# Attention with two gated layers on one core: softmax sums inverted for two head pairs at once, and the first values kept on chip

## The chip, the cores and the metric

The kernel runs on one core of a Trainium2 chip. The metric is device time in microseconds (us), the median of a few runs of the whole kernel in one launch. The core's engines are called here as the profile calls them: PE (TensorE matmuls, with PEld for its weight loads), DVE (VectorE), ACT (ScalarE), POOL (GpSimd) and SP (SyncE, which here only issues transfers). Each engine works through its own instruction stream in order, and waits at an instruction whose semaphores are not there yet.

## What is computed

The reference is windowed attention (batch 2, 8 heads, 768 positions, head size 64), then a dense gated layer, then a second layer in which each token goes to one of 8 experts:

```
keep   = is_global | is_local            # first 8 positions, or the last 96
scores = scale*q@k.T + bias;  a = exp(scores - max) where keep
x      = (a / (sum(a) + 1e-9)) @ v       # 1536 tokens x 512
x      = (silu(x @ w_gate) * (x @ w_val)) @ w_out        # 512 -> 1536 -> 512
e      = argmax(x @ r_gate);  out = gate * sigmoid * relu(x @ w1[e]) @ w2[e]
```

All inputs and the output are float32. In the kernel, large products are made of a high and a low part in the format fp32r, three matmuls for one.

## The kernel before

Queries come in 12 tiles of 128 positions, six for each of the two batches; tile i is position tile t = i % 6 of batch i // 6. Because a query only looks at the last 96 positions and at the first few, a tile needs its own keys and those of the tile before (two blocks of 128), and the first 8 positions of the batch. The kernel doesn't give these first positions a block of their own. It writes the first GW = 32 keys and values of the batch over the first 32 rows of the *previous* tile's block, which lie too far back to be local for this tile. A table of biases (`tabs`) is built for that layout. So from the second tile of a batch on, two things are put in place for each tile: keys (L324 to L328, on POOL, from the copy `kgb` that was taken at the batch's first tile) and values (L390 to L391, by a transfer from HBM on SP's queue, 32 partitions x 8 heads x 64 values).

Work goes in steps: one step is one tile and one pair of heads, 48 in all. What belongs to a step is spread over five:

- `att_S` (step s): scores into two PSUM banks `ps_s0`, `ps_s1`; DVE adds the bias and takes the maximum (L346, as a minimum of negated scores) into the buffer `sp`; ACT takes the exponential and its sum `sm` (L350).
- `att_R` (s + 1): DVE adds 1e-9 to two sums (L378, shown as L174 `rs`), inverts them (L379), and POOL multiplies `sp` by the result (L380).
- `att_P` (s + 3): PE transposes `sp` (L365), ACT or DVE copies it to `pT`.
- `att_V` (s + 4): PE multiplies by the values (L396). After the fourth pair `att_X` writes the tile's tokens as `xhi` (ACT, L402) and `xlo` (DVE, L403).

Tiles 0 and 1 (8 steps) run first with filler matmuls (`spin`, L149). Then, after a pause of 4 steps (GO = 12), the first dense layer runs between the attention steps: its up-products (L446) and down-products (L478 to L480) are handed out in small portions, and in the same stretch DVE and ACT turn that layer's wide weights into float32 and split them (`wide_to_f32` and `split_raw`, L411 to L429; a unit is a piece of weights of 128 x 1024). The first up-products need `xhi` and `xlo` of tiles 0 and 1 and the first two units. Seven units fit beside attention; the others are converted when attention's memory is free. Most instructions' order on an engine is set by a scheduler that goes by its own estimate of when each is ready; those wrapped in `pin` keep their written order. Buffers matter too: `sp` has 4, `rs`, `pT` and `qr` have 2, the values `vr` have 3.

Of the kernel before, what the change touches and what calls it, by code (L numbers as in the profile page):

```python
# [20 lines left out]
P = 128  # L21
BIG = 1.0e30
GW = 32
# [10 lines left out]
def attn_moe_moe_kernel(  # L34
# [138 lines left out]
    def ts(o, a, s1, s2, o0, o1=ALU.bypass):  # L173
        return nc.vector.tensor_scalar(out=o, in0=a, scalar1=s1, scalar2=s2, op0=o0, op1=o1)  # L174
# [143 lines left out]
    def att_S(i, j):  # L318
        b, t = bt(i)
        sl, order, tb = window(i)  # L320
        nw = len(order) * P
        if j == 0 and t > 0:
            o = (i - 1) % 3
            if stacked(i):  # L324
                nc.gpsimd.tensor_copy(ks[:, o, :, 0:GW], f(kg))
            else:
                nc.gpsimd.tensor_copy(khi[:, o, :, 0:GW], f(kgh))
                nc.gpsimd.tensor_copy(klo[:, o, :, 0:GW], f(kgl))  # L328
# [41 lines left out]
            nc.vector.tensor_copy(pT[:, :, 0:n, :], pt[:, :, 0:n, :])  # L370
        pt_t[(i, j)] = pT

    def att_R(i, j):
        sl, order, tb = window(i)
        nw = len(order) * P
        sp = sp_t[(i, j)]
        rs = at_p.tile([P, 2, 1], F32, tag="rs", name="rs")
        ts(rs[:, :, 0], sm[:, i, 2 * j:2 * j + 2], 1e-9, None, ALU.add)  # L378
        nc.vector.reciprocal(rs, rs)  # L379
        nc.gpsimd.tensor_tensor(out=sp[:, :, 0:nw], in0=sp[:, :, 0:nw], in1=rs.to_broadcast([P, 2, nw]), op=ALU.mult)  # L380

    av_t = {}

    def att_V(i, j):
        b, t = bt(i)
        sl, order, tb = window(i)
        pT = pt_t.pop((i, j))
        if j == 0:
            av_t[i] = ps_tile("av", [P, NPAIR, P])
            if t > 0:  # L390
                nc.sync.dma_start(out=v_t[i - 1][0:GW], in_=v[b, :, 0:GW, :].rearrange("h p d -> p h d"))  # L391
        av = av_t[i]
        for w, src in enumerate(order):
            vt = v_t[i] if src == 0 else v_t[i - 1]
            for e in range(2):
                nc.tensor.matmul(av[64 * e:64 * e + 64, j, :], vt[:, 2 * j + e, :], pT[:, e, w, :],  # L396
                                 start=(w == 0), stop=(w == len(order) - 1))
# [465 lines left out]
    for t in range(nstep + PAUSE + 5):  # L863
        rate = (0, 0, 0) if t < GO else (1, 0, 1 + (t % 3 == 2))
        nspin = 0 if t >= GO else 10 if t < 3 else 5 if t < FIRST else 8
        new, norm, turn, mul = (step_at(t - z) for z in (0, 1, 3, 4))
        if norm:
            att_R(*norm)
        if t < NPAIR:
            scale_tab(t, 0)  # L870
        if TL <= t + 1 < NPAIR + TL:
            scale_tab(t + 1 - TL, 1)
        if new:
            att_S(*new)
        quanta(rate[0])
        spin(nspin)
        if mul:
            att_V(*mul)
            if mul[1] == NPAIR - 1:
                i = mul[0]  # L880
                att_X(i)
                if i % 2 == 1:
                    ready.add(i // 2)
                if i + 2 < NTILE:
                    load_v(i + 2)
        quanta(rate[1])
        if turn:
            att_P(*turn)
        quanta(rate[2])
        spin(nspin)  # L890
        if new and new[0] != 1:
            transposes(*new)
        elif FIRST <= t < FIRST + 2:
            transposes(1, t - FIRST)
        if t < GO:
            early(t)
        elif t < GO + 2 * NE and (t - GO) % 2 == 0:
            clear_rows((t - GO) // 2)
        elif t == GO + 2 * NE:
            split_wr()  # L900
            nc.gpsimd.tensor_copy(ids[:, NTILE - 1:NTILE], tokid[:, NTILE - 1:NTILE])
# [455 lines left out]
```

## Time and profile before

| what | us |
|---|---|
| median of 3 runs (lowest, highest) | 667.36 (666.58, 669.77) |
| the profiled execution's own time | 666.85 |
| its span on the core | 665.0 |
| PE busy, of the span | 634.8 (95%) |
| DVE busy | 437.2 (66%) |
| ACT busy | 325.6 (49%) |
| POOL busy | 134.2 (20%) |

Busy times are those of the whole span, which has several stages. Attention with its start lies between 0 and about 200 us; then come the rest of the first dense layer (to about 460 us), the routing, and the experts. A busy PE need not be at its peak, because matmuls overlap. The profile's waits name who ended an idle stretch of an engine; an idle stretch in square brackets, as [0.72 <-PE ps_s L338], stands in a timeline's row behind the instruction that followed it.

### The profile page before, as it was taken

What the parts mean: (1) busy time and instruction counts of PE and PEld (TensorE: products, weight loads), DVE (VectorE), ACT (ScalarE), POOL (GpSimd) and SP (SyncE); (2) the same over time, 40 slices, a digit from 0 to 9 for tenths busy, and PEclk for the clock granted to TensorE, in tenths of its full rate; (3) what the DMA queues carried; (4) which work ended last, traced back from release to release, by engine and by line L of the source; (5) the groups of instructions that cost most, each with busy time, mean ns of one, the idle gap of its engine ahead of it and who ended that gap; (6) DMA issues with size and microseconds to landing.
All of it is one profiled execution on the core that took longest, in us unless ns stands there. A gap on an engine that the chain in (4) does not pass through costs nothing.

```text
span 665.0 us, 11812 instructions
## 1 busy us (share of the span) xinstructions
PE 634.8 (95%) x4455; PEld 549.8 (83%) x4455; DVE 437.2 (66%) x1087; ACT 325.6 (49%) x755; POOL 134.2 (20%) x180
## 2 busy tenths in 40 slices
PE   9899999999999999999999999998979999999993
PEld 8777678888888798999999999986867888888882
DVE  6899985666677898464464535556579777876330
ACT  4777866666665553131132222233467666766230
POOL 3404644444432420000000111001311100110011
PEclk9899999999999999999999999999999999999998
DMA  8679982210015535030010111113689767662001
GB/s 219 164 196 257 191 187 64 65 36 21 22 25 192 175 129 203 1 127 1 1 65 1 63 64 64 49 61 99 204 292 316 223 234 246 221 219 95 12 27 30
DMA packets 71587, 80.84 MB, mean 122 GB/s; under 512 B 43376, under 2 KB 43376, under 8 KB 71520
## 3 DMA queue, kind: packets, MB, share of 16 engines
q1 hardware_dynamic: 64960, 57.35, 30.6%
q0 software_dynamic: 6560, 22.64, 10.1%
q8 instruction: 37, 0.61, 0.4%
q14 instruction: 30, 0.25, 0.1%
HBM read 66.31 MB, written 14.26 MB: 121 GB/s over the span
## 4 chain that ended last, share of the span: by engine, by line
PE 71%; DVE 11%; DMA 7%; issue 5%; ACT 4%; POOL 1%; POOLq 0%; SPq 0%; DVEq 0%; ACTq 0%
PE ps_gv L446 25%; PE ps_gv L971 5%; PE ps_av L396 3%; DMA raw<-in_moe_w_dram 2%; PE ps_y L480 2%; PE ps_y L971 2%; PE ps_s L971 2%; PE ps_y L479 2%; PE ps_tr L365 2%; PE ps_y L478 2%; PE ps_s L989 2%; PE ps_s L990 2%; PE ps_s L988 2%; PE ps_s L334 2%; DMA raw<-in_moe_w_val_dram 2%
## 5 line engine op out<-in xcount | busy, mean ns | idle before, releaser
L446 PE MATMUL ps_gv<-xlo,whi 128*128 128x256 f32 x576 | 164.5, 286 | 0.9 <-DVE xlo L403 0.9
L446 PE MATMUL ps_gv<-xhi,whi 128*128 128x256 f32 x576 | 164.8, 287 | 0.3 <-DVE hh L454 0.2
L446 PE MATMUL ps_gv<-xhi,wlo 128*128 128x256 f32 x576 | 164.8, 286 | 0.0
L446 PEld LDWEIGHTS ps_gv<-xlo,whi 128*128 128x128 f32 x576 | 110.0, 191 | 4.7 <-DVE xlo L403 1.3
L446 PEld LDWEIGHTS ps_gv<-xhi,whi 128*128 128x128 f32 x576 | 109.7, 191 | 4.5 <-ACT xhi L402 0.5
L446 PEld LDWEIGHTS ps_gv<-xhi,wlo 128*128 128x128 f32 x576 | 110.2, 191 | 1.5 <-issue 0.3
L635 DVE TENSOR_TENSOR wlo<-raw,whi 128x512 fp32r<-128x512 f32 (+1 forms) x104 | 81.2, 811 | 17.1 <-ACT whi L632 15.0
L632 ACT CAST whi<-raw 128x512 fp32r<-128x512 f32 (+1 forms) x104 | 71.0, 720 | 33.3 <-PE ps_s L990 11.6
L453 DVE SCALAR_TENSOR_TENSOR hh<-th,ps_gv 128x256 f32<-128x256 f32 x72 | 30.1, 418 | 75.3 <-ACT th L451 75.3
L451 ACT ACTIVATE th<-ps_gv 128x256 f32<-128x256 f32 x72 | 27.5, 382 | 88.4 <-PE ps_gv L446 88.2
L380 POOL TENSOR_TENSOR sp<-sp,rs 128x512 f32<-128x512 f32 (+1 forms) x48 | 47.7, 994 | 85.5 <-DVE rs L379 70.1
L457 ACT CAST hi<-hh 128x256 fp32r<-128x256 f32 x72 | 29.2, 405 | 56.8 <-DVE hh L454 52.8
L350 ACT ACTIVATE sp<-sp,mn 128x256 f32<-128x256 f32 (+1 forms) x96 | 46.7, 487 | 19.5 <-DVE mn L346 12.6
L606 POOL DMA_INDIRECT xs<-ypay,rw x12 | 13.0, 1080 | 206.8 <-DVE rw L177 189.2
L346 DVE CUSTOM_DVE_ANT_0 sp<-ps_s,tabs 128x256 f32<-128x256 f32 (+1 forms) x96 | 36.1, 391 | 6.0 <-PE ps_tr L365 3.6
L480 PE MATMUL ps_y<-whi,lo 128*128 128x512 f32 x96 | 38.3, 406 | 1.7 <-POOL lo L458 1.6
L478 PE MATMUL ps_y<-whi,hi 128*128 128x512 f32 x96 | 38.8, 405 | 0.3
L479 PE MATMUL ps_y<-wlo,hi 128*128 128x512 f32 x96 | 38.5, 401 | 0.0
L653 POOL DMA_INDIRECT out_dram<-ot,idt x14 | 13.9, 990 | 116.9 <-ACT ot L994 88.4
L971 PE MATMUL ps_gv<-xx,whi 128*128 128x448 f32 x112 | 36.1, 372 | 0.4 <-DVE hs L973 0.4
L396 PE MATMUL ps_av<-pT,vr 128*64 128x128 f32 x352 | 29.8, 287 | 1.3 <-DMA vr<-in_v_dram 1.3
L454 DVE SCALAR_TENSOR_TENSOR hh<-hh,ps_gv 128x256 f32<-128x256 f32 x72 | 29.9, 415 | 1.0
(265 smaller groups left out, 1403.7 us busy)
## 6 DMA issues: line engine op xcount, KB each, us to landing
raw<-in_moe_w_dram SPq DMA_DIRECT2D x30, 1024.0 KB, 5.3
xs<-ypay SPq DMA_DIRECT2D x8, 514.0 KB, 9.0
raw<-in_moe_w_out_dram POOLq DMA_DIRECT2D x4, 1024.0 KB, 5.8
xr<-xs POOLq DMA_DIRECT2D x7, 449.8 KB, 5.8
ytok<-ypay SPq DMA_DIRECT2D x12, 257.0 KB, 3.2
ypay<-in_k_dram SPq DMA_DIRECT2D x12, 256.0 KB, 4.9
qr<-in_q_dram SPq DMA_DIRECT2D x12, 256.0 KB, 4.4
vr<-in_v_dram SPq DMA_DIRECT2D x12, 256.0 KB, 4.3
```

The lines of the kernel that those rows point to most:

```text
L346: nc.vector.tensor_tensor_reduce(out=sp[:, e, 0:nw], in0=pS[e][:, 0:nw], in1=tb[:, h0 + e, :], scale=-QS, scalar=3.0e38, op0=ALU.add, op1= ...
L350: nc.scalar.activation(out=sp[:, e, 0:nw], in_=sp[:, e, 0:nw], func=AF.Exp, bias=mn[:, i, h0 + e:h0 + e + 1], scale=-1.0, accum_out=sm[:, ...
L380: nc.gpsimd.tensor_tensor(out=sp[:, :, 0:nw], in0=sp[:, :, 0:nw], in1=rs.to_broadcast([P, 2, nw]), op=ALU.mult)
L396: nc.tensor.matmul(av[64 * e:64 * e + 64, j, :], vt[:, 2 * j + e, :], pT[:, e, w, :], start=(w == 0), stop=(w == len(order) - 1))
L446: nc.tensor.matmul(o, a[:, kk, fo:fo + P], x[c][:, kk, :], start=(kk == 0 and m == 0), stop=(kk == KD - 1 and m == 2))
L453: nc.vector.scalar_tensor_tensor(out=hh, in0=th, scalar=1.0, in1=pg[:, 0, :], op0=ALU.add, op1=ALU.mult)
L478: nc.tensor.matmul(o, hi[:, sl], wh, start=first, stop=False)
L479: nc.tensor.matmul(o, hi[:, sl], wl, start=False, stop=False)
L480: nc.tensor.matmul(o, lo[:, sl], wh, start=False, stop=last)
L632: ins = nc.scalar.copy(hv[:, o], raw[:, o])
L635: nc.vector.tensor_tensor(out=lv[:, o], in0=raw[:, o], in1=f(hv[:, o]), op=ALU.subtract)
L971: nc.tensor.matmul(d, a[:, kk, c], x, start=(kk == 0 and m == 0), stop=(kk == KD - 1 and m == 1))
```

## The change

Three edits, all in attention.

1. `att_R` can take two pairs at once (n = 2). From step GO on it is called at odd pairs only: one add and one reciprocal over four sums, and then the two multiplications on POOL, one behind the other. The earlier of the two pairs is so inverted a step later than before. Tiles 0 and 1 keep one pair at a time.
2. At the first tile of a batch POOL copies the first 32 rows of its values into a new tile `vg`, in two halves: heads 0 to 3 into partitions 0 to 31, heads 4 to 7 into partitions 32 to 63. From the third tile of the batch on (t > 1) two POOL copies put them over the first 32 rows of the previous tile's values, in place of the transfer on SP's queue. At t = 1 the previous tile is the batch's first, whose rows are the right ones already, and nothing is put in place.
3. The keys' copies too are left out at t = 1 and stay for t > 1.

So 20 of 48 adds and 20 of 48 reciprocals go from DVE; 10 transfers go from SP's queue; POOL loses 3 key copies (two at tile 1, one at tile 7) and gains 4 copies that fill `vg` and 16 that put the values in place.

```
-        if j == 0 and t > 0:
+        if j == 0 and t > 1:
             o = (i - 1) % 3
...
-    def att_R(i, j):
+    def att_R(i, j, n=1):
...
-        sp = sp_t[(i, j)]
-        rs = at_p.tile([P, 2, 1], F32, tag="rs", name="rs")
-        ts(rs[:, :, 0], sm[:, i, 2 * j:2 * j + 2], 1e-9, None, ALU.add)
+        rs = at_p.tile([P, 2 * n, 1], F32, tag="rs", name="rs")
+        ts(rs[:, :, 0], sm[:, i, 2 * j:2 * (j + n)], 1e-9, None, ALU.add)
         nc.vector.reciprocal(rs, rs)
-        nc.gpsimd.tensor_tensor(out=sp[:, :, 0:nw], in0=sp[:, :, 0:nw], in1=rs.to_broadcast([P, 2, nw]), op=ALU.mult)
+        for z in range(n):
+            sp = sp_t[(i, j + z)][:, :, 0:nw]
+            nc.gpsimd.tensor_tensor(out=sp, in0=sp, in1=rs[:, 2 * z:2 * z + 2].to_broadcast([P, 2, nw]), op=ALU.mult)
...
+    vg = at_p.tile([P, H // 2, HD], F32, name="vg", bufs=1)
...
-            if t > 0:
-                nc.sync.dma_start(out=v_t[i - 1][0:GW], in_=v[b, :, 0:GW, :].rearrange("h p d -> p h d"))
+
+            if t == 0:
+                for z in range(2):
+                    nc.gpsimd.tensor_copy(vg[z * GW:(z + 1) * GW], v_t[i][0:GW, z * NPAIR:(z + 1) * NPAIR])
+            elif t > 1:
+                for z in range(2):
+                    nc.gpsimd.tensor_copy(v_t[i - 1][0:GW, z * NPAIR:(z + 1) * NPAIR], vg[z * GW:(z + 1) * GW])
...
-        if norm:
+        if norm and t < GO:
             att_R(*norm)
+        elif norm and norm[1] % 2 == 1:
+            att_R(norm[0], norm[1] - 1, 2)
```

The edits also move instructions, because the scheduler places everything anew. Three places matter below.

POOL, from the first multiplication of attention to the key copies of tile 3. L380 (L381 in the changed kernel) is the multiplication, 128x2x128 for tile 0 and 128x512 later; L327 and L328 put the keys in place; L458 (L465) is the low part in the dense layer. Before:

```order
L380 TENSOR_TENSOR sp<-sp,rs 128x2x128 x3
L328 CAST kbuf<-kgb 128x4x32
L327 CAST kbuf<-kgb 128x4x32
L380 TENSOR_TENSOR sp<-sp,rs 128x2x128
L380 TENSOR_TENSOR sp<-sp,rs 128x512 x2
L328 CAST kbuf<-kgb 128x4x32
L327 CAST kbuf<-kgb 128x4x32
L380 TENSOR_TENSOR sp<-sp,rs 128x512 x3
L458 TENSOR_TENSOR lo<-hh,hi 128x256
L380 TENSOR_TENSOR sp<-sp,rs 128x512
L328 CAST kbuf<-kgb 128x4x32
L327 CAST kbuf<-kgb 128x4x32
```

The same place in the changed kernel, where L398 is the copy of values:

```order
L381 TENSOR_TENSOR sp<-sp,rs 128x2x128 x4
L381 TENSOR_TENSOR sp<-sp,rs 128x512 x2
L328 CAST kbuf<-kgb 128x4x32
L327 CAST kbuf<-kgb 128x4x32
L381 TENSOR_TENSOR sp<-sp,rs 128x512 x2
L398 COPY vr<-vg 32x256 x2
L465 TENSOR_TENSOR lo<-hh,hi 128x256
L381 TENSOR_TENSOR sp<-sp,rs 128x512 x2
L328 CAST kbuf<-kgb 128x4x32
L327 CAST kbuf<-kgb 128x4x32
```

The key copies of tile 1 are gone from among the multiplications of tile 0. Those of tiles 2 and 3 stand where they stood, and the first copies of values (for tile 2) stand behind the multiplications of tile 1.

DVE, around the end of tile 1 (L403, L410 in the changed kernel, writes `xlo`). L412, L417, L420 and L429 (7 more in the changed kernel) are a unit's conversion in that order, and L346 is the first pair of tile 2. Before:

```order
L429 TENSOR_TENSOR wlo<-raw,whi 128x1024
L412 TENSOR_SCALAR raw<-raw 128x1024
L346 ISA sp,mn<-ps_s_779,tabs 128x256
L346 ISA mn 128x1
L417 SCALAR_TENSOR_TENSOR raw<-raw 128x1024
L346 ISA sp,mn<-ps_s_780,tabs 128x256
L346 ISA mn 128x1
L420 SCALAR_TENSOR_TENSOR raw<-raw 128x1024
L403 TENSOR_TENSOR xlo_87<-ps_av,xhi_81 128x4x128
L243 TENSOR_TENSOR kbuf<-ps_tr,kbuf 128x512
L429 TENSOR_TENSOR wlo<-raw,whi 128x1024
```

In the changed kernel:

```order
L436 TENSOR_TENSOR wlo<-raw,whi 128x1024
L419 TENSOR_SCALAR raw<-raw 128x1024
L424 SCALAR_TENSOR_TENSOR raw<-raw 128x1024
L410 TENSOR_TENSOR xlo_87<-ps_av,xhi_81 128x4x128
L427 SCALAR_TENSOR_TENSOR raw<-raw 128x1024
L346 ISA sp,mn<-ps_s_779,tabs 128x256
L346 ISA mn 128x1
L346 ISA sp,mn<-ps_s_780,tabs 128x256
L346 ISA mn 128x1
L243 TENSOR_TENSOR kbuf<-ps_tr,kbuf 128x512
L436 TENSOR_TENSOR wlo<-raw,whi 128x1024
```

`xlo` of tile 1 has moved ahead of one conversion pass and of the maxima of tile 2's first pair.

SP, the transfers from the third unit of weights on (L106 loads keys and queries, L112 values, L123 weights, L391 puts the first values in place). Before:

```order
L123 DMA raw<-in_moe_w_out_dram 128x2x1024
L391 DMA vr<-in_v_dram 32x8x64
L106 DMA ypay<-in_k_dram 128x8x64
L106 DMA qr<-in_q_dram 128x8x64
L123 DMA raw<-in_moe_w_gate_dram 128x4x512
L112 DMA vr<-in_v_dram 128x8x64
L391 DMA vr<-in_v_dram 32x8x64
L123 DMA raw<-in_moe_w_val_dram 128x4x512
```

In the changed kernel:

```order
L123 DMA raw<-in_moe_w_out_dram 128x2x1024
L106 DMA ypay<-in_k_dram 128x8x64
L106 DMA qr<-in_q_dram 128x8x64
L123 DMA raw<-in_moe_w_gate_dram 128x4x512
L112 DMA vr<-in_v_dram 128x8x64
L106 DMA ypay<-in_k_dram 128x8x64
L123 DMA raw<-in_moe_w_val_dram 128x4x512
```

The loads behind a L391 no longer stand behind its wait for the products that still read those rows.

## Rows read from the trace of the kernel before

**Rows 1.** Windows: start:end, length; busy us (instructions) by engine; PEclk, DMA share, GB/s.

```profile
17.00:45.00 28.00, 24.71 (x260) 19.83 (x257) 24.53 (x57) 20.19 (x47) 7.69 (x10) 0.94 0.66 157
45.00:97.00 52.00, 49.11 (x363) 38.19 (x364) 49.44 (x119) 36.59 (x90) 25.07 (x27) 1.00 0.98 230
97.00:200.00 103.00, 101.82 (x818) 85.19 (x818) 66.31 (x232) 66.62 (x187) 43.80 (x56) 1.00 0.17 38
```

**Rows 2.** Timeline, 17 to 19.7 us: start us, us, engine, line, operation.

```profile
17.90 0.75 POOL L328 CAST kbuf<-kgb 128x128 fp32r<-128x128 f32 x1
18.60 0.29 POOL L327 CAST kbuf<-kgb 128x128 fp32r<-128x128 f32 x1
18.94 0.62 PE L338 MATMUL ps_s<-kbuf,qbuf 64*128 64x256 f32 x6 [1.43 <-POOL kbuf L327]
19.59 0.42 DVE L346 CUSTOM_DVE_ANT_0 sp<-ps_s,tabs 128x256 f32<-128x256 f32 x1 [0.72 <-PE ps_s L338]
```

**Rows 3.** Timeline, 27 to 46 us: the values of tile 1 and the first up-products.

```profile
28.25 0.46 SPq L391 DMA_DIRECT2D vr<-in_v_dram  x1
...
34.81 1.09 PE L396 MATMUL ps_av<-pT,vr 128*64 128x128 f32 x16
...
39.66 1.23 DVE L420 SCALAR_TENSOR_TENSOR raw<-raw 128x1024 int32<-128x1024 int32 x1
...
40.79 0.69 DVE L403 TENSOR_TENSOR xlo<-ps_av,xhi 128x512 fp32r<-128x512 f32 x1
...
41.54 0.39 PE L446 MATMUL ps_gv<-xlo,whi 128*128 128x256 f32 x1 [0.85 <-DVE xlo L403]
```

**Rows 4.** Source view of L391, 28 to 29 us: its one transfer there.

```profile
DMA to landing us min/median/max: 5.2/5.2/5.2
```

**Rows 5.** Timeline, 84 to 93 us: the values of tile 5.

```profile
85.09 0.57 SPq L391 DMA_DIRECT2D vr<-in_v_dram  x1
...
91.66 0.66 PE L396 MATMUL ps_av<-pT,vr 128*64 128x128 f32 x8 [1.27 <-DMA vr<-in_v_dram]
```

**Rows 6.** Lines by form, DVE, 45 to 97 us: busy us, mean ns | idle before.

```profile
L417 DVE SCALAR_TENSOR_TENSOR raw<-raw 128x1024 int32<-128x1024 int32 x6 | 9.7, 1613 | 0.1
L420 DVE SCALAR_TENSOR_TENSOR raw<-raw 128x1024 int32<-128x1024 int32 x6 | 9.1, 1514 | 0.0
L429 DVE TENSOR_TENSOR wlo<-raw,whi 128x1024 fp32r<-128x1024 f32 x4 | 6.1, 1514 | 1.0 <-ACT whi L428 1.0
L412 DVE TENSOR_SCALAR raw<-raw 128x1024 int32<-128x1024 int32 x5 | 4.9, 979 | 0.0
...
L174 DVE TENSOR_SCALAR rs<-sm 128x2 f32<-128x2 f32 x13 | 2.9, 223 | 1.3 <-ACT sp L350 1.2
...
L379 DVE RECIPROCAL rs<-rs 128x2 f32<-128x2 f32 x13 | 2.0, 154 | 0.0
```

**Rows 7.** Timeline, 45 to 100 us, DVE and POOL: alone and beside one another.

```profile
60.13 0.15 DVE L174 TENSOR_SCALAR rs<-sm 128x2 f32<-128x2 f32 x1
60.20 0.41 DVE L346 CUSTOM_DVE_ANT_0 sp<-ps_s,tabs 128x256 f32<-128x256 f32 x1
...
62.49 1.04 POOL L380 TENSOR_TENSOR sp<-sp,rs 128x512 f32<-128x512 f32 x1 [0.60 <-DVE rs L379]
62.57 2.04 DVE L417 SCALAR_TENSOR_TENSOR raw<-raw 128x1024 int32<-128x1024 int32 x1
...
69.01 0.67 DVE L412 TENSOR_SCALAR raw<-raw 128x1024 int32<-128x1024 int32 x1
...
84.75 1.23 DVE L417 SCALAR_TENSOR_TENSOR raw<-raw 128x1024 int32<-128x1024 int32 x1
```

**Rows 8.** Lines by form, POOL, 17 to 200 us.

```profile
L325 POOL CAST kbuf<-kgb 128x256 fp32r<-128x256 f32 x5 | 2.0, 397 | 6.2 <-PE ps_s L334 6.2
```

**Rows 9.** Timeline, 156 to 170 us: multiplication and transposes of step 37.

```profile
157.39 1.04 POOL L380 TENSOR_TENSOR sp<-sp,rs 128x512 f32<-128x512 f32 x1 [1.15 <-DVE rs L379]
...
169.33 0.49 PE L365 MATMUL ps_tr<-ident,sp 128*128 128x128 f32 x3
```

## Prediction

> **What bounds the kernel now.** I read the table of windows first, then the chain of waits and PE's list of waits for the stretch that the edits touch, then timelines at the places that these named. Attention falls into three parts [rows 1]. From 17 to 45 us no engine is full: PE is busy 24.7 of 28.0 us, much of it filler, and DVE 24.5. From 45 to 97 us two engines are nearly full: DVE 49.4 of 52.0 us, PE 49.1. In this part DVE converts weights beside attention. From 97 to 200 us PE is busy 101.8 of 103.0 us, DVE only 66.3. What is worth something is therefore a wait of PE before 97 us, or time of DVE before 97 us; after that only PE's own work counts, and the edits don't change it.
>
> That attention's other engines run ahead of PE in the third part shows in one step [rows 9]: POOL ends its multiplication at 157.39 + 1.04 = 158.43 us, and PE transposes the result at 169.33, 10.9 us later. A step there takes about 4 us (103.0 us for some 25 steps).
>
> **The change part by part.** The sum is made against the profiled execution's own 666.85 us, of which 665.0 is the span; the median of the runs is 667.36, 0.5 higher.
>
> *Keys of tile 1.* PE waits 1.43 us for L327, whose two copies for tile 1 end at 18.89, and DVE waits 0.72 us for the scores that follow [rows 2]. Without the copies PE can go on at once, and DVE is held by its conversion pass until about 18.9. I take DVE's 0.7 as the gain, since PE only runs filler otherwise; the ends are 0 and 1.4. What is late next there is DVE itself.
>
> *Values of tile 1.* The transfer is issued at 28.25 and takes 5.2 us to land [rows 3, 4], so at 33.5; PE multiplies by these rows at 34.81. In the new kernel the rows are right already, and the products can follow their transposes. `xlo` of tile 1 starts on DVE at 40.79, and the first up-product that needs it has been waited for 0.85 us at 41.54 [rows 3]. In the new order of DVE it stands ahead of L420, which costs 1.13 us from start to start (39.66 to 40.79), and of two maxima. So `xlo` could come 1.1 to 2.1 us earlier. But DVE has the same conversions to do, and PE soon needs the units after; I take 0.6, with 0 and 2.0 as ends.
>
> *Fewer adds and reciprocals.* DVE has 13 of each between 45 and 97 us [rows 6], nearly all of which become half as many: 6.5 of each less. Their busy time overstates them: an add at 60.13 lasts 0.15 us, but the next instruction starts 0.07 us later [rows 7], and with a reciprocal of the same kind a pair costs about 0.15 us of DVE. That is 6.5 x 0.15 = 1.0 us. The adds last 223 ns in the mean, 70 ns more than that one, because some are held up by POOL; half of 13 x 0.07 gives 0.4 more. Together 1.4; the ends are 0.5 (where DVE only waits for the same sums elsewhere) and 2.5 (half of 2.9 + 2.0 us of busy time [rows 6]). The 14 pairs or so after 97 us are hidden by PE.
>
> *The pair's second multiplication, and the first a step later.* Both are covered in the third part: of 10.9 us the earlier pair loses a step of 4 us, the later one 1.04. In the second part the cover is smaller, since there PE follows POOL more closely; the scheduler has moved the transposes of tile 2's first pair behind the scores of another step. I count nothing, and a loss of at most 1 us.
>
> *Values of the later tiles.* For tile 5 the transfer is issued at 85.09, and PE waits 1.27 us for it at 91.66 [rows 5]. The copy that replaces it is split by heads, so that heads 0 to 3 can be replaced while heads 4 to 7 of the same block are still read. Gain 1.3, ends 0 and 1.5. The other eight transfers are waited for nowhere in PE's list.
>
> *POOL's new work.* No row shows a copy from `vg`. The nearest is L325, a copy of 256 elements on 128 partitions, 397 ns [rows 8]. Four tiles (2 to 5) have two such copies each before 97 us: 8 x 0.397 = 3.2 us more on POOL, less 0.75 + 0.29 = 1.0 for the keys of tile 1 [rows 2]; 2.1 net. POOL has room: 25.1 of 52.0 us [rows 1]. But its work costs DVE. An L417 that ran beside a multiplication took 2.04 us, one that ran alone 1.23 [rows 7]: 0.81 us lost to an operation of 1.04. Over the part, against 1.23 alone for L417, L420 and L429 and 0.67 for L412, DVE lost 6 x 0.38 + 6 x 0.28 + 4 x 0.28 + 5 x 0.31 = 6.7 us, and 0.9 in the adds: 7.6 us for POOL's 25.1, or 0.30 per us. So 2.1 x 0.30 = 0.6 us of loss. Ends: 0, and 3.2 x 0.81 / 1.04 = 2.5 if every copy meets a conversion.
>
> The Trainium skill (SBUF — State Buffer, "SBUF: two separate sides") has it that VectorE and GpSimd share a pair of ports under an exclusive lock that is held for a whole instruction, which speaks against putting copies on GpSimd. By that rule each copy would cost whatever conversion it meets its whole length, the far end above; the row with 2.04 us agrees that the loser stands still, and the mean of 0.30 says how seldom it is met.
>
> The Trainium skill (DMA: Bandwidth & Descriptors, "Anatomy of one DMA") gives a transfer some 2.0 us plus its bytes over 436 GB/s, so as an estimate 2.2 us for the 64 KB of values. By that the transfers removed would have been cheap; here they took 5.2 us and, at tile 5, 6.5, beside others, and the measurement decides.
>
> *Queues.* SP loses ten transfers that each waited for products to end; loads of keys and weights behind them can go earlier. With DMA's share at 0.98 in the second part [rows 1] an earlier issue gains little. I count nothing.
>
> The sum: -0.7 - 0.6 - 1.4 - 1.3 + 0.6 = -3.4 us, or 666.85 - 3.4 = 663.45 for a profiled execution. Against the median of the runs that is 664.0, and this is what I predict.
>
> **The rivals.** A measurement of this kernel can tell 0.5%, 3.3 us, from no change; my forecast lies just at that edge.
>
> *PE bounds the second part already.* PE is busy 49.1 of 52.0 us there, and busy time says nothing of whether it could go faster. If PE isn't held by DVE, what DVE saves there is lost: only PE's own waits go, the 1.27 us of tile 5 and perhaps 0.7 at the start. Then 667.36 - 1.3 to 2.0 = about 665.7. For it: DVE's list names few waits of PE. Against it: DVE has only 2.6 us free in 52.
>
> *The new waits replace the old.* The copies of values stand in POOL's in-order stream between pairs of multiplications, which wait for sums. If the products of a tile's first pair then wait for the copy about as long as for the transfer, the 1.3 and the 0.6 are gone and 2.1 - 0.6 = 1.5 is left: 665.9. The split by heads speaks against it.
>
> *DVE is locked out (slower).* Two multiplications in a row hold DVE's conversion for 2.08 us where one held it 1.04, and behind the conversion stand the maxima for which PE's next scores wait, because each score bank exists once. If each of the 6.5 double multiplications and all copies cost the second part that much, the loss is 6.5 x 1.04 + 2.5 = 9.3 us against gains of 4.0: 672.6. It decides the sign as soon as the lock costs DVE over 4.0 us more than before in that part. Against it: the total of multiplications is the same, and their stretches are half as many.
>
> *The whole start moves.* If DVE's and PE's waits before 45 us are one chain, the gains there are 1.4 + 2.0 in place of 1.3, and with the upper ends of the rest (2.5 + 1.5) it is -7.4: 660.0.
>
> **How the numbers follow.** The forecast has 0.50, PE bounding the second part 0.24, new waits 0.08, the lock-out 0.11, the start as one chain 0.07. The forecast's own range, 2 to 5 us of gain, is 662.4 to 665.4; of its 0.50 I put 0.40 beyond 0.5%, given that the edge falls within it and that the gains not counted (queues, fewer waits) outnumber the losses. Faster is then 0.40 + 0.07 = 0.47; same 0.10 + 0.24 + 0.08 = 0.42; slower 0.11. The range for 8 in 10 runs from 660.8 to 668.4: it takes in both rivals without a gain, some of the upper ends, and a small loss through the lock.
>
> **What would show it.** Right: in the new trace PE has no wait for POOL at 18 us and none for values near 90; the first up-product that needs `xlo` starts 1 to 3 us before 41.5; DVE's L174 and L379 are 28 each in all; DVE's conversions (L417, L420 there under new numbers) keep means near 1.6 and 1.5 us; the last product with values comes about 3 us earlier than the 200 us of before, and everything behind it is shifted by that and not changed. Wrong: if the last product with values isn't earlier though DVE's busy time has gone down, PE was the bound; if the conversions' means rise to 1.9 us or more, the lock ate the gain; if PE waits for POOL's copies at a tile's first product, the new wait took the place of the old; if the time from 200 us on changes by more than 1 us, something that I left out is at work.

## The result: 8 us slower, and the profile after

The changed kernel takes 675.14 us in the median of 4 runs (674.19 to 677.4), the kernel before 666.97 beside it (666.13 to 669.77). The ratio is 1.0121, with a 95% interval of 1.0093 to 1.015. The profiled execution has a span of 675.6 us against 665.0, at a mean granted clock of 0.982 against 0.993. It was the slowest of the four (677.4 us), so its lengths lie some 2 us above the median's.

Line numbers of the new kernel: L381 multiplies on POOL, L395 fills `vg`, L398 puts values in place; L403 are the products with values, L410 writes `xlo`, L453 are the up-products; a unit's conversion is L419, L424, L427, L436 (L412, L417, L420, L429 before).

The start moved as the edits promise. The timeline has the first scores of tile 1 at 17.56 us and no wait there (18.94 in [rows 2]), `xlo` of tile 1 at 37.79, and the first up-product that needs it at 38.53 (41.54 in [rows 3]):

```profile
17.56 0.74 PE L338 MATMUL ps_s<-kbuf,qbuf 64*128 64x256 f32 x6
...
37.79 0.68 DVE L410 TENSOR_TENSOR xlo<-ps_av,xhi 128x512 fp32r<-128x512 f32 x1
...
38.53 0.39 PE L453 MATMUL ps_gv<-xlo,whi 128*128 128x256 f32 x1 [0.41 <-DVE xlo L410]
```

The windows, with the columns of [rows 1], show where the time went. In the second part PE's busy time has gone from 49.11 to 44.34 us and its granted clock from 1.00 to 0.88. The last two rows split the place: PE is idle for a quarter of 73 to 85 us, and from 85 to 98.6 us it works at a granted clock of 0.50, that is at 1.2 GHz. In the changed kernel:

```profile
17.00:45.00 28.00, 26.32 (x270) 21.02 (x269) 25.68 (x60) 21.30 (x50) 8.94 (x10) 1.00 0.73 171
45.00:97.00 52.00, 44.34 (x290) 33.63 (x290) 43.54 (x97) 33.09 (x81) 26.50 (x28) 0.88 0.78 213
97.00:200.00 103.00, 101.84 (x798) 84.61 (x797) 59.76 (x195) 64.50 (x180) 44.86 (x65) 0.99 0.16 37
73.00:85.00 12.00, 9.21 (x73) 6.33 (x71) 11.86 (x21) 8.47 (x21) 8.06 (x9) 1.00 0.86 237
85.00:98.60 13.60, 11.49 (x53) 9.24 (x55) 9.16 (x25) 5.76 (x16) 3.42 (x5) 0.50 0.35 120
```

The kernel before in the last two of these windows:

```profile
73.00:85.00 12.00, 10.81 (x81) 7.42 (x80) 11.49 (x30) 9.83 (x27) 7.19 (x8) 1.00 0.95 226
85.00:98.60 13.60, 12.31 (x106) 10.16 (x104) 11.47 (x29) 7.53 (x20) 6.11 (x6) 1.00 0.80 189
```

PE's list of waits (us in total, times, longest) has one long wait that is new, and no transfer of values any more (1.27 us in [rows 5]):

```profile
PE ps_tr L365 <- DVE qbuf L243: 3.5, 1, 3.5
PE ps_s L338 <- POOL kbuf L327: 2.1, 2, 1.3
```

The second row is new in this part as well: at 55 and 72 us PE's scores wait for key copies that stand behind two multiplications on POOL. The kernel with edit 1 alone has these two waits too (1.7 us) and isn't slower.

The timeline at that wait, from 79.3 to 86 us (L225 transposes tile 5's queries, L242 and L243 write their high and low parts, and the next transposes L365 need the same bank):

```profile
79.58 0.60 PE L225 MATMUL ps_tr<-ident,qr 128*128 128x128 f32 x4
80.03 0.98 POOL L123 DMA_DIRECT2D raw<-in_moe_w_out_dram  x1 [1.40 <-DVE rs L174]
80.21 0.59 ACT L242 CAST qbuf<-ps_tr 128x512 fp32r<-128x512 f32 x1
80.46 3.18 DVE L419 TENSOR_SCALAR raw<-raw 128x1024 int32<-128x1024 int32 x1
81.04 2.04 POOL L381 TENSOR_TENSOR sp<-sp,rs 128x512 f32<-128x512 f32 x2
...
83.75 1.35 DVE L424 SCALAR_TENSOR_TENSOR raw<-raw 128x1024 int32<-128x1024 int32 x1
85.02 0.68 DVE L243 TENSOR_TENSOR qbuf<-ps_tr,qbuf 128x512 fp32r<-128x512 f32 x1
85.75 0.48 PE L365 MATMUL ps_tr<-ident,sp 128*128 128x128 f32 x1 [3.55 <-DVE qbuf L243]
```

The low part could start when ACT's L242 ends, at 80.8. It starts at 85.02, because two conversion passes stand ahead of it in DVE's stream. Both belong to weight unit 7 (the load of `w_val` issued at 71.48), and nothing needs unit 7 before attention's memory is free (DVE writes the next low part of weights at 212.95). Before, one pass over unit 6 stood there, and PE waited 0.6 us:

```profile
79.97 1.56 DVE L429 TENSOR_TENSOR wlo<-raw,whi 128x1024 fp32r<-128x1024 f32 x1 [0.40 <-ACT whi L428]
81.45 0.68 DVE L243 TENSOR_TENSOR qbuf<-ps_tr,qbuf 128x512 fp32r<-128x512 f32 x1
82.19 0.65 PE L365 MATMUL ps_tr<-ident,sp 128*128 128x128 f32 x4 [0.58 <-DVE qbuf L243]
```

So DVE spends the time on work that isn't due, PE stands, and PE's clock falls.

The clock's part, as an estimate from the rows: 13.6 us at 0.50 do at most what 6.8 us at 1.00 would, and PE is idle for 2.1 of them. From step 15 to step 18 the changed kernel takes 4.0 us longer than the kernel before (17.8 against 13.8, table below). The Trainium skill (TensorE: Matmul & The Clock Gate, "HAM oscillation — how this bites in real kernels") has it that a wait of PE lets the clock fall and that the work behind the wait pays; the trace agrees with 3.55 us of wait and 0.50 behind it.

The last product with values starts at 210.60 us, 9.9 later than before, and the span is 10.6 longer: from there on 0.7 us more. Of the 9.9 us, 7.6 are there at step 18 (103.6 us against 96.0). The other 2.3 come between step 18 and the last product, with the clock at 1.00; the last section of the experiments comes back to them.

### The profile page after: what moved, and what is told of

It is laid out like the page before. It is cut to its first block, busy times and chain, and to the rows that moved or that the text cites. A ratio compares the mean times of both kernels' runs of the same rounds, so it can differ in the third digit from the quotient of the medians.

```text
span 675.6 us, 11720 instructions
## 1 busy us (share of the span) xinstructions
PE 642.1 (95%) x4455; PEld 554.9 (82%) x4455; DVE 430.8 (64%) x1047; ACT 325.7 (48%) x755; POOL 143.3 (21%) x197
## 5 line engine op out<-in xcount | busy, mean ns | idle before, releaser
L453 PE MATMUL ps_gv<-xhi,whi 128*128 128x256 f32 x576 | 166.4, 289 | 0.9 <-DVE hh L461 0.6
L453 PE MATMUL ps_gv<-xlo,whi 128*128 128x256 f32 x576 | 165.5, 287 | 0.4 <-DVE xlo L410 0.4
L453 PE MATMUL ps_gv<-xhi,wlo 128*128 128x256 f32 x576 | 164.7, 286 | 0.0
L453 PEld LDWEIGHTS ps_gv<-xhi,whi 128*128 128x128 f32 x576 | 110.5, 192 | 6.5 <-DVE hh L461 0.8
L453 PEld LDWEIGHTS ps_gv<-xlo,whi 128*128 128x128 f32 x576 | 110.6, 192 | 4.2 <-issue 0.7
L453 PEld LDWEIGHTS ps_gv<-xhi,wlo 128*128 128x128 f32 x576 | 110.9, 193 | 0.8
L458 ACT ACTIVATE th<-ps_gv 128x256 f32<-128x256 f32 x72 | 27.6, 384 | 94.3 <-PE ps_gv L453 94.1
L381 POOL TENSOR_TENSOR sp<-sp,rs 128x512 f32<-128x512 f32 (+1 forms) x48 | 49.6, 1049 | 38.7 <-DVE rs L378 31.6
L346 DVE CUSTOM_DVE_ANT_0 sp<-ps_s,tabs 128x256 f32<-128x256 f32 (+1 forms) x96 | 35.6, 392 | 13.0 <-PE ps_s L334 3.8
L660 POOL DMA_INDIRECT out_dram<-ot,idt x14 | 13.6, 973 | 117.0 <-ACT ot L1003 88.4
L403 PE MATMUL ps_av<-pT,vr 128*64 128x128 f32 x352 | 30.4, 290 | 1.6 <-ACT pT L368 1.0
```

The lines of the kernel that those rows point to most:

```text
L346: nc.vector.tensor_tensor_reduce(out=sp[:, e, 0:nw], in0=pS[e][:, 0:nw], in1=tb[:, h0 + e, :], scale=-QS, scalar=3.0e38, op0=ALU.add, op1= ...
L381: nc.gpsimd.tensor_tensor(out=sp, in0=sp, in1=rs[:, 2 * z:2 * z + 2].to_broadcast([P, 2, nw]), op=ALU.mult)
L453: nc.tensor.matmul(o, a[:, kk, fo:fo + P], x[c][:, kk, :], start=(kk == 0 and m == 0), stop=(kk == KD - 1 and m == 2))
```

## Experiments

Ratios are against the kernel before, run on the same chip; differences in us between two experiments are of medians, which can come from different chips. The table has the start of the first up-product, the first transposes of steps 8, 12, 15 and 18, and the last product with values, in us.

| kernel | first up | step 8 | step 12 | step 15 | step 18 | last |
|---|---|---|---|---|---|---|
| before | 39.6 | 49.1 | 70.2 | 82.2 | 96.0 | 200.7 |
| changed | 37.6 | 52.4 | 70.3 | 85.8 | 103.6 | 210.6 |
| e1 edits 2, 3 alone | 37.6 | 48.0 | 69.1 | 83.3 | 96.6 | 205.1 |
| e2 edit 1 alone | 38.4 | 52.5 | 70.1 | 81.8 | 94.8 | 198.7 |
| e9 changed, units 7 and 8 later | 37.1 | 52.0 | 69.2 | 80.8 | 94.0 | 201.1 |
| e13 skip at the second tile alone | 37.1 | 47.7 | 69.0 | 81.7 | 94.6 | 199.7 |
| e14 as e1, short copies | 37.4 | 47.9 | 68.8 | 82.5 | 97.0 | 205.4 |
| e17 as e9, copies on ACT | 37.0 | 51.7 | 69.1 | 80.6 | 93.6 | 201.0 |

### The edits apart (e1, e2)

```
e1:     if norm: att_R(*norm)                        # as before
...
e2:     if j == 0 and t > 0: ...                     # keys as before
        ...
        if t > 0: nc.sync.dma_start(out=v_t[i - 1][0:GW], ...)
```

> Only edits 2 and 3 (first values kept on chip, no copies at the second tile); every pair is inverted by itself, as before. Theory A (the two multiplications in a row lock DVE, a query tile's low part comes late, PE idles 3.55 us and the granted clock then stays at 1.2 GHz for 13.65 us): none of that happens, the terms of the prediction without the sums are left, -0.7 - 0.6 - 1.3 + 0.6 = -2.0 us, so 665 us, PE's longest wait between 75 and 100 us under 2 us, and no stretch of 1.2 GHz there. Rival B (the copies of values on POOL are to blame): 672 us or more, with a wait of PE over 3 us and the low clock behind it.

Measured: 671.45 us, ratio 1.0071 (1.0042 to 1.0101). PE waits 2.2 us for L243 at 81 us.

> Only edit 1 (sums inverted for two pairs at once); keys and values are put in place as before, by copies and by transfers. Theory A in its wide form (double multiplications cost wherever they stand): 672 to 676 us, conversions' means in the second part as long as in the changed kernel. Theory A in its narrow form (they cost only where a low part of a query tile stands behind locked conversion passes; here the order has it ahead of them): 665 to 668 us, and no low clock between 80 and 100 us. Rival B: 666 us, and nothing late.

Measured: 664.99 us, ratio 0.9984 (0.9956 to 1.0013). Apart, the edits give +4.9 and -1.5 us, 3.4 together; the changed kernel lost 8.2. My theory A, that the double multiplications lock DVE, expected the loss with the pairing. It came with the other edits, and more of it where both are in. The table shows too that the pair's later inversion delays step 8 by 3.4 us and that nothing is left of that at step 12.

### The lock, taken away (e3, e4)

```
e3:     m = 8 if n == 2 and i * NPAIR + j == 16 else nw     # columns of L381
...
e4:     m1_load: nc.sync if n < 9 else nc.gpsimd             # was n < 8
```

> The changed kernel with the same instructions in the same order on every engine; only the two multiplications of tile 4's first two pairs work on 8 columns instead of 256 of each head, so those weights stay unnormalised in part. Theory A: the pass beside them takes 1.7 us or less in place of 3.18, the low part of the query tile starts 1.5 to 2.5 us earlier, PE waits 1.5 us or less before the transposes of step 15, the granted clock stays at 2.4 GHz, and the time falls to 666 to 669 us. Rival C (the order of DVE's instructions alone makes the wait, with or without the lock): the wait stays over 3 us and the time at 673 to 676 us. Rival E (the low clock has another cause): the wait shrinks and the low clock stays, 671 to 674 us.

Measured: 674.3 us, ratio 1.0107 (1.0078 to 1.0136). The pass takes 0.68 us, L243 starts at 81.53, and PE's wait there is 0.92. But the time stays nearly as it was. The timeline of this kernel shows why:

```profile
79.61 0.68 DVE L421 TENSOR_SCALAR raw<-raw 128x1024 int32<-128x1024 int32 x1
...
81.53 0.68 DVE L243 TENSOR_TENSOR qbuf<-ps_tr,qbuf 128x512 fp32r<-128x512 f32 x1
82.27 0.66 PE L365 MATMUL ps_tr<-ident,sp 128*128 128x128 f32 x4 [0.92 <-DVE qbuf L243]
...
88.17 0.70 DVE L421 TENSOR_SCALAR raw<-raw 128x1024 int32<-128x1024 int32 x1 [3.54 <-DMA raw<-in_moe_w_out_dram]
89.26 1.14 PE L338 MATMUL ps_s<-kbuf,qbuf 64*128 64x256 f32 x5 [3.79 <-DVE mn L346]
```

The next pass in DVE's stream, the first over unit 8, stands ahead of the maxima of the next scores and waits for its transfer, which the source view of L123 times from POOL's issue:

```profile
DMA to landing us min/median/max: 9.0/9.0/9.0
```

PE then waits 3.79 us for those maxima, and its clock falls at 89 us instead of 85. So the narrow theory A falls as well: a faster pass only moves the wait to the next place where the same order bites.

> The changed kernel, but the ninth transfer of weights (the first that POOL issues, at 80.03 us, for 0.98 us) is issued by SP. DVE's order up to the late low part is the same. If the issue on POOL holds DVE's pass like a multiplication does, the pass of 3.18 us takes 2.2 us, PE's wait of 3.55 us becomes 2.5 us, and the time is 666 to 675 us by whether the clock still falls. If only the multiplications hold it, the pass keeps 3.0 to 3.2 us, and wait, low clock and time stay as they are (674 to 676 us).

Measured: 671.64 us, ratio 1.0089 (1.005 to 1.0127): 3.5 us less than the changed kernel by the medians, with overlapping intervals. The pass takes 1.43 us, PE waits 2.3, and the stretch at 0.50 is 6.8 us long in place of 13.65. So what holds DVE's passes at this place may be part of the loss, and not most of it. That POOL's issue itself holds the pass isn't shown: in e3 the pass took 0.68 us beside the issue (79.17 to 80.44 us), and here it also meets the multiplications at another moment.

### The order: units 7 and 8 held back (e5 to e8)

```
        for x in (a, b) if late else ():        # first passes of ACT and DVE
            tc.add_manual_dep(x.ins, late.ins.name, ...)
        ...
        wide_to_f32(raws.pop(n), n < 6, xl[4] if n in (7, 8) else None)   # xl[4]: xlo of tile 4
```

> The changed kernel; the first passes (ACT and DVE) over weight units 7 and 8, whose results nothing needs before 200 us, may not start before the low part of tile 4's tokens (about 105 us). DVE's order is the same up to the late low part of tile 5's queries, which then follows the maxima at once. Theory F (the loss is the order: passes over units that aren't needed yet stand ahead of the low part and ahead of maxima, one of them behind its transfer): no wait of PE over 2 us between 75 and 100 us, no 1.2 GHz there, last product with values before 201 us, and 661 to 665 us. Theory A (locked passes): the double multiplications are all there, 670 us or more. Rival B (copies of values on POOL cost by themselves): 668 us or more.

Measured: 669.13 us, ratio 1.0026 (1.0007 to 1.0045), 6 us better than the changed kernel. Step 18 comes at 93.7 us, ten earlier. PE is busy 24.46 of 25 us from 75 to 100, but only 47.58 of the next 50:

```profile
75.00:100.00 25.00, 24.46 (x189) 19.03 (x188) 15.32 (x45) 16.03 (x43) 12.62 (x19) 1.00 0.64 175
100.00:150.00 50.00, 47.58 (x363) 39.20 (x362) 34.18 (x99) 32.94 (x89) 22.87 (x29) 1.00 0.21 49
```

There the held passes fall due together: from 104.56 us the first passes of both units (2.15 us) stand ahead of a copy of `pT` that PE waits for (0.55 us). The hold costs by itself:

> The kernel before with the same hold of units 7 and 8. Theory F: the order there has the low part of tile 5's queries ahead of these passes already, so little is won: 664 to 667 us. If the hold by itself is worth as much as in the changed kernel, 658 to 661 us; then the changed kernel lost nothing special and both suffer from these passes.

Measured: 671.42 us, ratio 1.0064 (1.0037 to 1.009): against both expectations slower, by 4.5 us.

> Only edit 1 (two pairs at once), with the hold of units 7 and 8. Its order has the low part ahead of the passes without the hold. Theory F: as without the hold or up to 2 us better, 662 to 665 us. If double multiplications cost wherever they stand: over 667 us.

Measured: 668.53 us, ratio 1.0024 (1.0006 to 1.0042), 3.5 us slower than without the hold.

> Only edits 2 and 3 (first values kept on chip), with the hold of units 7 and 8; the pass over unit 6 still stands ahead of the low part. Theory F: 5 us or more better than without the hold (671.5), 662 to 666 us. Rival B (the copies on POOL themselves): within 2 us of 671.5.

Measured: 672.82 us, ratio 1.008 (1.0054 to 1.0106). No gain: the pass over unit 6 stays ahead of the low part, and PE waits 1.5 us there. So a hold to 105 us mends the place at 80 and makes another.

### The order alone (e9, e10)

The same hold, but only until the low part of tile 5's queries:

```
        wide_to_f32(raws.pop(n), n < 6, xl[5] if n in (7, 8) else None)   # xl[5]: L243 of tile 5
```

> The changed kernel; the first passes over weight units 7 and 8 may not start before the low part of tile 5's queries on DVE. That alone puts DVE's order from there on into that of the kernel with edit 1 alone, which took 665 us: low part, one pass, maxima, two passes, and unit 8's first pass behind its transfer. Theory F (the loss of 8 us is this order, and what PE's wait does to the granted clock): 662 to 666 us, no wait of PE over 2 us between 75 and 100 us and no 1.2 GHz there. Rival B (copies of values on POOL cost by themselves, wherever the passes stand): 668 to 672 us, with the loss spread over the tiles from 100 us on.

Measured: 666.79 us, ratio 0.9997 (0.9976 to 1.0019). This is the decisive run: all three edits, all double multiplications and all copies are there, and the loss of 8.2 us is gone (8.3 less than the changed kernel's median). One of its twelve executions took 676.64 us at a mean granted clock of 0.977, so the low clock isn't shut out. The tie moves little else: counted in the two traces, all but 16 of DVE's 1047 instructions and all but 15 of PE's 4455 stand in the changed kernel's order. In its timeline (line numbers are one higher here) DVE waits 0.35 us for ACT, writes the low part, and takes the long pass behind it:

```profile
78.53 0.60 PE L226 MATMUL ps_tr<-ident,qr 128*128 128x128 f32 x4
...
79.83 0.69 DVE L244 TENSOR_TENSOR qbuf<-ps_tr,qbuf 128x512 fp32r<-128x512 f32 x1 [0.35 <-ACT qbuf L243]
79.98 2.04 POOL L382 TENSOR_TENSOR sp<-sp,rs 128x512 f32<-128x512 f32 x2
80.56 2.04 DVE L420 TENSOR_SCALAR raw<-raw 128x1024 int32<-128x1024 int32 x1
80.77 0.60 PE L366 MATMUL ps_tr<-ident,sp 128*128 128x128 f32 x4
```

The pass ends 0.6 us behind the double multiplication, and PE doesn't wait for it. The window that stood at 0.50 is at 1.00:

```profile
85.00:98.60 13.60, 13.38 (x110) 11.23 (x111) 11.90 (x29) 7.93 (x22) 7.06 (x9) 1.00 0.45 128
```

From step 18 on the tie changes nothing: 107.1 us to the last product, 107.0 in the changed kernel.

> Only edits 2 and 3 (first values kept on chip), with the same order laid on units 7 and 8. Unit 6's last pass stays ahead of the low part, as in the kernel before. Theory F: 663 to 667 us in place of 671.5. Rival B: 669 to 672 us.

Measured: 671.09 us, ratio 1.0079 (1.0052 to 1.0105). Rival B's number: with single pairs this order isn't most of what costs (PE still waits 1.5 us for L244 behind unit 6's pass, and 1.3 us for maxima).

### Later pairs (e11, e12)

```
        if norm and t < 17:        # was t < GO (12)
```

> The changed kernel, but tile 2 keeps one pair at a time (pairs only from tile 3 on); nothing is laid on the units. In the changed kernel the transposes of step 8 came 3.3 us later than before (52.4 against 49.1), which I put to the first pair's wait for its partner. If so, they come at 48 to 49 us here, and the 2 to 3 us won at the start are still there at step 12. DVE's order has the low part behind unit 6's last pass, as before: 662 to 666 us by theory F, 668 us or more by rival B.

Measured: 671.42 us, ratio 1.0087 (1.0055 to 1.0119); step 8 at 48.7 us.

> Only edit 1, and that only from tile 3 on. Transposes of step 8 at 49 to 50 us in place of 52.5. If waiting for the partner cost the kernel with edit 1 some 2 us, 662 to 664 us; if the stretch to step 12 is set by the units' conversion, so that what is late at step 8 is caught up, 664 to 666 us as with edit 1 alone.

Measured: 667.07 us, ratio 1.0008 (0.9991 to 1.0025); step 8 at 47.9 us. Against e2 step 8 comes 4.6 us earlier, step 12 only 0.9, and the time is no shorter: what waiting for the partner costs at step 8 is caught up anyway. e11 is 3.7 us better than the changed kernel, in an order with one pass ahead of the low part (PE waits 1.4 us there) and no low clock, but far from e9.

### What of edits 2 and 3 costs (e13 to e18)

```
e13:    if j == 0 and t > 1: (keys)     if t > 1: nc.sync.dma_start(...)     # before + skip
e14:    tensor_copy(v_t[i - 1][0:GW, z * NPAIR:z * NPAIR + 1, 0:8], ...)       # e1 + short copies
e15:    e13 with edit 1                 e16:    e2 with t > 1 for the keys
e17:    e9 with nc.scalar.copy for L398 e18:    e9 with the short copies of e14
```

> The kernel before, but at the second tile of a batch neither keys nor values are put in place (the rows are right already); for the later tiles keys are copied and values come by transfer, as before. This is the start's part of edits 2 and 3 without the copies on POOL. By my terms (-0.7 and -0.6) 665.5 us. If the 4.4 us that edits 2 and 3 lost together come from the copies, 664 to 666 us; if they come from the moved start (PE's order behind it), 669 to 671 us.

Measured: 666.01 us, ratio 1.0001 (0.9983 to 1.0019). The skip costs nothing and brings nothing that the runs can tell, though the first up-product starts at 37.1.

> Edits 2 and 3 as in the run of these alone (671.5 us), with PE's and DVE's instructions in the same order; only the copies that put values in place are 8 columns of one head instead of 64 of four, so the first values of later tiles are wrong. If the copies cost by their own length (POOL busy, DVE held), 667 to 669 us. If the loss is the order and the moved start, within 1.5 us of 671.5.

Measured: 669.33 us, ratio 1.0048 (1.0029 to 1.0066). Against the kernel before beside each, e1 lost 4.9 us and e14 3.1, so 1.8 may be the copies' length (the intervals overlap). 3.3 us against e13 are left. PE waits 2.1 us for L243 and its clock falls, as in e1; yet step 18 is only 2.4 us later than in e13, and the last product 5.7.

> Edit 1 and the second tile's skip of keys and values, with transfers for the later tiles: the changed kernel without its copies of values. DVE's order has the low part of tile 5's queries ahead of the passes. If edit 1 (-1.5) and the skip (-1.3) add up, 663 to 664.5 us, the best so far. If the moved start costs what edits 2 and 3 lost, 667 to 670 us.

Measured: from 662.99 to 676.01 us, median 672.35, ratio 1.0099 (1.0064 to 1.0134). The six executions lie too far apart to price the edits by. The mean granted clock goes along with the time: 0.992 at 662.99 us, 0.978 at 671.68, 0.971 at 676.01. As an estimate, the clock's difference between the first two, 0.014 of 665 us, is 9.3 us, and they lie 8.7 apart. The best execution is no better than the best of the kernel before (663.15). What PE does where the clock falls isn't shown, since the profiled execution was the one of 662.99.

> Edit 1 and the skip of the keys alone; values come by transfer at every tile from the second on. PE loses its wait of 1.43 us for POOL at 18 us and keeps the products of tile 1 behind their transfer. If the early products of tile 1 are what disturbs the order, this stays good: 663.5 to 665.5 us. If any earlier start is lost again, 665 us as with edit 1 alone.

Measured: 664.93 us, ratio 0.9977 (0.9957 to 0.9998), the only interval of eighteen wholly below 1, by 0.2%, which by itself shows little.

> The changed kernel with units 7 and 8 held until the low part of tile 5's queries (666.8 us so), and the copies that put values in place made by ACT instead of POOL. If half of what the copies cost is POOL's time beside DVE, as the 2.2 us of the short copies say, and ACT has room (about 50% busy), 664 to 665.5 us, a version faster than the kernel before. If the copies only cost by when the values are in place, 666 to 668 us.

Measured: 666.27 us, ratio 1.0002 (0.9982 to 1.0022).

> The same with the copies on POOL, but 8 columns of one head long, so that first values of later tiles are wrong; PE's and DVE's order is that of the run with 666.8 us. If the copies' length costs here as it did with single pairs, 664 to 665 us; if the hold has taken that cost away too, 666 to 667.5 us.

Measured: 665.98 us, ratio 0.9987 (0.9972 to 1.0003). Neither differs from e9. With the order mended, the copies' length is worth 0.8 us by the medians, less than the runs can tell.

What costs is what the table shows behind step 18. From there to the last product the kernels that place values by a transfer take 103.9 to 105.1 us (before, e2, e12, e13, e15, e16), and those that place them by a copy and hold nothing to 105 us take 105.8 to 108.5 (the changed kernel, e1, e3, e4, e9, e10, e11, e14, e17, e18), also where the copies are short (e14, e18) or on ACT (e17). In e2 and in e9, with the columns of [rows 1]:

```profile
94.80:198.70 103.90, 102.92 (x830) 86.44 (x828) 64.52 (x208) 66.75 (x187) 45.78 (x58) 1.00 0.17 38
94.00:201.10 107.10, 105.99 (x839) 87.78 (x837) 64.46 (x210) 67.84 (x189) 48.83 (x69) 1.00 0.15 33
```

The 3.2 us are PE's own busy time: PE is idle for 1.0 and 1.1 us, and the clock is at 1.00. Edit 2 thus takes some 3 us more in the stretch that PE bounds, and the 2.0 us by which e9 is ahead of the kernel before at step 18 are gone at the last product. At most seven of e9's matmuls are up-products that e2 does later (as an estimate 0.9 us). PE's instructions come in another order there (counted in the traces of e2 and e9, some 300 of 4455 stand elsewhere); what of that order costs isn't shown.

## Why the prediction was wrong

I forecast 664.0 us, in a range up to 668.4. The step that failed is the sum itself from 45 to 97 us, the part where conversion and attention overlap: it prices each edit in the order of the kernel before and has no term for the new order. The one place that names a move is "the pair's second multiplication, and the first a step later", where I saw that the scheduler had moved the transposes of tile 2's first pair and counted "nothing, and a loss of at most 1 us". I read the new order of DVE only up to tile 2, and the moves didn't end there. At tile 5 the new order puts two passes over unit 7 ahead of the low part, and one over unit 8 ahead of maxima. That is worth 8.3 us (the changed kernel against e9): PE waits 3.55 us, and then runs at 0.50. The pairing alone doesn't make this order (e2 loses nothing), and the other edits alone make a milder one (in e1 one pass over unit 7 and one over unit 6 stand there, and PE waits 2.2 us).

A second step failed behind it: "after that only PE's own work counts, and the edits don't change it". From step 18 to the last product the changed kernel takes 107.0 us against 104.7. In e9 this takes back what the start had won.

The terms of the sum:

- Keys and values of tile 1, -0.7 and -0.6. Both waits went, and the first up-product that needs `xlo` came 3.0 us earlier, more than my far end of 2.0. But at step 12 it is 0.1 us later than before, and e13, which has only this, measured -0.2 us (interval -1.1 to +1.3). I had the place right and took a gain at the start for one at the end. What takes it back isn't shown; DVE's conversions, which I named as late next, are one candidate, and the pair's delay at step 8 (3.4 us in e2) another in the changed kernel.
- Fewer adds and reciprocals, -1.4. The adds of the changed kernel take 176 ns in the mean, 223 before [rows 6]. Edit 1 alone measured -1.5 (interval by the ratio -2.9 to +0.9). It agrees, and the interval doesn't exclude nothing.
- Values of tile 5, -1.3. The wait for the transfer is gone, but it is gone in e2 too, which keeps the transfers, so the copies can't be credited with it.
- POOL's new work, +0.6, far end 2.5. The short copies say 1.8 with single pairs and 0.8 with the order mended, both with overlapping intervals. The size fits the range, but not the 4.9 us that edits 2 and 3 cost alone (e1).

The rivals. "DVE is locked out" came nearest in time, 672.6, and is wrong in its mechanism. The conversions' means did not rise to 1.9 us:

```profile
L427 DVE SCALAR_TENSOR_TENSOR raw<-raw 128x1024 int32<-128x1024 int32 x6 | 8.3, 1377 | 0.0
L424 DVE SCALAR_TENSOR_TENSOR raw<-raw 128x1024 int32<-128x1024 int32 x5 | 7.2, 1432 | 0.5 <-ACT raw L418 0.3
L419 DVE TENSOR_SCALAR raw<-raw 128x1024 int32<-128x1024 int32 x5 | 6.4, 1290 | 0.6 <-DMA raw<-in_moe_w_val_dram 0.6
...
L174 DVE TENSOR_SCALAR rs<-sm 128x4 f32<-128x4 f32 x6 | 1.1, 176 | 0.0
```

L424 and L427 are shorter than L417 and L420 were [rows 6]; only L419 is longer, mostly through the one pass of 3.18 us. e3 took the long multiplications away there and got 0.8 us by the medians, e4 moved POOL's issue and got 3.5; e9 left both and got 8.3. "The new waits replace the old" was the right kind of answer with the wrong wait: I looked for it at POOL's copies, and it was mainly a DVE pass that no edit touches. "PE bounds the second part" doesn't explain this result: PE was busy there for 44.34 us of 52.

Of the signs I had listed, the early `xlo`, the missing waits at 18 and 90 us and the unchanged time behind the last product (0.7 us more) came true. PE does wait for POOL's copies at two first scores, but of keys and not of values. "The last product isn't earlier though DVE's busy time has gone down" came true too (DVE 43.54 us in the second part, 49.44 before), and my reading of it, that PE was the bound, was wrong: both engines were idle more.

Edits 2 and 3 alone cost 4.9 us with single pairs. Of that, the skip is nothing that can be told (e13) and the copies' length 1.8 at most by the medians (e14). In the profile most of it comes behind step 18: 0.6 us later there than before, 4.4 at the last product (e1). e10, with the order at tile 5 held, has the same stretch (107.6 us), so that order alone couldn't bring its loss back. Open is what in PE's order makes this stretch longer. The clock may add to it in the other runs: the mean granted clock was 0.9885 in the median of e1's runs and 0.9855 in e10's, against 0.991 and 0.992 for the kernel before beside them, as an estimate 1.7 and 4.3 us of 665. No profile here shows where it fell in e10's other runs.

## What to carry to other kernels

Where a scheduler places instructions anew, a small edit is priced in the new order of every engine, all the way through: look for work that isn't due standing ahead of work that is waited for, above all a pass that itself waits for a transfer. That holds for the engine that is the bound as well: in the same stretch of steps PE was busy 103 us in one order and 106 in another, with hardly a wait in either. An engine's spare work needs a tie that keeps it behind the critical instruction, and the tie is to be as short as possible: held to the low part it gave 8.3 us, held 25 us longer 6.0, and in kernels without the fault the long hold cost 3.5 to 4.5. A gain near the start of a pipeline is worth what is left of it where the next stretch is bound.

## What the runs showed that I had not expected

- A PE wait can be paid twice. In all five profiles with a wait of over 2 us between 80 and 90 us (the changed kernel, e1, e3, e4, e14) the granted clock fell to 0.50 during the wait or within 2.1 us of its end; with 1.4 to 1.5 us it fell in one (e8) of three (e8, e10, e11); where PE waited less, it stayed at 1.00 there. It can also fall with less: in the profile of e18 it is 0.50 from 56.6 to 77 us, after a stretch in which PE was busy 9.57 of 11.6 us and waited 1.3 us at most. That execution took 674.23 us, where the median is 665.98; in e9, with PE's and DVE's instructions in the same order, PE was busy 10.04 us of this stretch and the clock stayed. In e18:

```profile
45.00:56.60 11.60, 9.57 (x61) 7.15 (x60) 10.37 (x22) 7.79 (x17) 6.27 (x6) 1.00 0.91 249
56.60:77.00 20.40, 20.40 (x81) 15.59 (x81) 10.44 (x28) 9.12 (x21) 9.06 (x10) 0.50 0.57 155
```

- One kernel's executions can spread by 2% (e15), more than any edit here is worth, and the mean granted clock goes along with them. That the clock is all of it is an estimate; only one of these executions has a trace.
- A pass of 0.68 us took 3.18 beside 3.02 us of POOL (0.98 for a transfer's issue, 2.04 for the double multiplication). The Trainium skill (SBUF — State Buffer, "Who interferes with whom") says that of DVE and GpSimd the one that comes first holds the shared ports for its whole instruction. The rows agree only in part: the pass started at 80.46, before the multiplications at 81.04, and still ended 0.56 us behind both of them, as it did behind both in e9; in e4 it ended during the second and took 1.43.
